# One gate group for the first two chunks, and first fills on VectorE, in a gated-recurrence and channel-mixer kernel

## The chip, the cores and the metric

The kernel runs on one core of a Trainium2 chip. The core has a matrix engine (TensorE, PE in the profile, its weight loads PEld), three elementwise engines (VectorE or DVE, ScalarE or ACT, GpSimd or POOL) and a queue engine (SyncE or SP) that here only issues DMAs. The metric is the device time in microseconds; a kernel's time is the median of its runs.

## The reference

Two blocks, one after the other, in float32 with the weights in float64.

```
# q, k, v, a_re, a_im: (B=4, H=8, S=768, D=48)
mag = sqrt(a_re^2 + a_im^2);  a = (a_re + i a_im) * min(mag, 0.999) / (mag + 1e-6)
for t in range(S):                       # per batch and head; state is D x D, complex
    S_re, S_im = a[t] * (S_re + i S_im)  # row d of the state is multiplied by a[t, d]
    S_re += outer(k[t], v[t])
    y[t] = q[t] @ S_re
x = y as (B, S, H*D = 384)
u = x + (x^T @ U @ V)^T                  # U: 768 x 32, V: 32 x 768, mixes along the sequence
out = u + relu(u @ w_ch1) @ w_ch2        # w_ch1: 384 x 1536, w_ch2: 1536 x 384
```

## The kernel before

The sequence is cut in chunks of 128 steps: six to a batch, 24 in all (`NT`). The recurrence inside a chunk becomes matrix products once the running products of the gates are known, so the work of a chunk has these parts.

- **Gates** (`gates`). From a_re and a_im ScalarE and VectorE make the logarithm of each gate's magnitude (`magnitudes`, 11 ScalarE and 5 VectorE operations on 384 values per chunk) and two exponentials of its sums over the chunk (`within`: one TensorE product `es ps`, two Exp). `totals` makes the decays of blocks of steps (`of_blocks`: TensorE products `tot`, one Exp into E, then four DMAs on SP's queue that copy E into T). `turns` and `angles` make the phases (Arctan, a TensorE prefix sum `ph`, rounding into F; chunk i of the first batch also adds the last row of F of chunk i-1) and `waves` the cosines and sines (`cs`).
- **Prep** (`prep`). VectorE multiplies q and k by the exponentials (L669) and by cs (L673, into QKC); TensorE transposes (L682) and ScalarE copies out (L685) into QK.
- **Chain** (`chain`). TensorE products of 32 columns (`inner`, L716), VectorE copies under a mask (L722) and multiplications of QK by T (L735 through the helper at L329), corners, state updates (G, GM) and y. This is ranked as "levels" and "rest".
- **Mixer** (`mixer`). When the six chunks of a batch are done, the mix along the sequence, and then for each pair of chunks the product with w_ch1 (`up`, L916), Relu, and the product with w_ch2 (`down`).

**Weights.** They arrive as float64. `single` takes one of 13 pieces (w1: 0 to 5, U and V: 6, w2: 7 to 12) through one of two raw buffers (a ring: pieces take them in their order), six VectorE operations (L486 to L496) and one accumulating DMA from GpSimd's queue (L499). `up` on the first half of its columns needs pieces 0 to 2, on the second half 3 to 5; the mix needs piece 6, `down` the rest.

**Groups and tables.** Gates are made in groups of chunks: before, chunk 0 alone, chunk 1 alone, then pairs. ScalarE's Exp and Ln need one activation table, Arctan and Sin another, so every group loads two (`switch`, L323, L1201 and L1210). In the plan a load writes a name that every table operation reads: it waits for all table operations declared ahead of it, and those declared after it wait for the load. The totals of chunk 0 are put off to the next group's Exp table (`later`, L1206). A group's gate tiles (ar, ai, x, y, n, z) are one buffer each, 768 values wide, handed from group to group; chunk 1's inputs therefore cannot be loaded before chunk 0's last reader is done.

**Order.** Every operation is declared with an engine, a cost, a rank and what it reads and writes. `Plan.order` then fixes one order for each engine: of the operations that are ready in its model, the one with the lowest rank goes first. Ranks come from the table `URGENCY` (per part and chunk), and for loads from a formula. SP and GpSimd's queues are in order too, so a DMA that waits holds back those behind it. Where TensorE has nothing to do before the first mixer, the plan puts in 128-wide products of the identity, called `spare` (L1232); they compute nothing that is used.

**First fills.** Ahead of the planned work GpSimd fills tiles with constants: total, ident, GL (L386), QKC (L392), three T (L400), two AT and two DG (L406, L407). VectorE fills only six columns of one value (L364). After that GpSimd makes `mid` (L415) and `total` (L435) from the loaded `prefix`.

Of the kernel before, what the change touches and what calls it, by code (L numbers as in the profile page):

```python
# [22 lines left out]
GC = 2  # L23
# [3 lines left out]
    "w1": {0: 577.09, 1: -1319.32, 2: 484.43, 3: -236.69, 4: 471.82, 5: -1058.73, 6: 187.51},  # L27
    "w2": {0: -111.09, 2: 522.21, 4: 896.97, 6: -52.37, 8: 604.14, 10: 640.8, 12: -317.28},
    "gates": {0: -265.04, 1: 268.17, 2: 43.76, 4: -996.63, 6: 89.37, 8: 509.61, 10: -55.71, 12: 809.99, 14: -95.12,
        16: 160.61, 18: -122.91, 20: -425.54, 22: -1729.17},  # L30
    "angles": {0: -126.72, 1: -84.17, 2: -1567.87, 4: -1150.68, 6: -325.13, 8: 105.31, 10: 61.73, 12: 732.88,
        14: -1148.2, 16: 655.25, 18: 538.84, 20: -116.45, 22: 233.15},
    "prep": {0: -1639.87, 1: -367.99, 2: -1022.47, 3: -12.47, 4: -106.92, 5: -436, 6: -74.87, 7: 260.1, 8: -1682.29,
        9: 278.7, 10: 47.08, 11: 569.46, 12: -1452.21, 13: -249.3, 14: -287.97, 15: -363.52, 16: -269.7,
        17: -1664.43, 18: -240.93, 19: 153, 20: -1089.48, 21: -198.95, 22: -127.5, 23: 757.32},
    "levels": {0: 731.75, 1: -318.03, 2: 17.02, 3: -430.68, 4: -436.08, 5: -170.38, 6: 221.56, 7: 124.72, 8: -1567.59,
        9: -1453.16, 10: -1698.36, 11: -60.78, 12: 502.58, 13: 523.21, 14: -1475.59, 15: 515.81, 16: -1265.88,
        17: 487.77, 18: -263.92, 19: 16.81, 20: 723.89, 21: -1759.83, 22: -1111.46, 23: -160.12},
    "rest": {0: 468.93, 1: -1086.12, 2: 24.25, 3: -218.54, 4: -1119.41, 5: -346.92, 6: 0.68, 7: -1700.8, 8: 681.55,
        9: -376.72, 10: -229.72, 11: -305.85, 12: -1069.62, 13: 601.71, 14: -282.72, 15: 204.95, 16: 59.77,  # L40
        17: 552.08, 18: -62.45, 19: 466.03, 20: -1105.96, 21: -351.77, 22: -1688.33, 23: 463.92},
# [147 lines left out]
def kernel(  # L189
# [47 lines left out]
    GROUPS = [(0, 1), (1, 2)] + [(n, n + GC) for n in range(2, NT, GC)]  # L237
    NG = len(GROUPS)

    PAIRED = 6  # L240
# [5 lines left out]
    AT_ONCE = (0, 1, 2, 3)  # L246
# [145 lines left out]
    nc.gpsimd.memset(QKC, 0.0)  # L392
# [5 lines left out]
    for n in range(3):  # L398
        TS.append(singles.tile([DQ, GC, H * NTOT], FP, name="T%d" % n))
        nc.gpsimd.memset(TS[n], 1.0)  # L400
    for n in range(3):
        VP.append(singles.tile([128, H, D], FP, name="VP%d" % n))
    for n in range(2):
        AT.append(singles.tile([128, H, HC], FP, name="AT%d" % n))
        DG.append(singles.tile([128, H, BLK], FP, name="DG%d" % n))
        nc.gpsimd.memset(AT[n], 0.0)  # L406
        nc.gpsimd.memset(DG[n], 0.0)  # L407
# [37 lines left out]
    def load_a(g):  # L445
        lo, hi = GROUPS[g]
        for nm, src in (("ar", a_re), ("ai", a_im)):
            for i in range(lo, hi):
                SP(c_dma(DM), ("load", (0, 0.5, 3)[g] if g < 3 else lo + 3), lambda nm=nm, src=src, i=i: nc.sync.dma_start(
                    out=get(nm, g)[:, i - lo], in_=rows(src, i)), writes=[(nm, g, i)])  # L450
# [80 lines left out]
    def gates(g):  # L531


        lo, hi = GROUPS[g]
        W = (hi - lo) * DM
        R1, R2 = ("gates", lo), ("angles", lo)
        ca, cd = c_act(W), c_dve(W)
        x, y, l, n, z, ar, ai = names = [(nm, g) for nm in ("x", "y", "l", "n", "z", "ar", "ai")]

        def t(b):  # L540
            a = get(*b)
            return (a.rearrange("p c h d -> p (c h d)") if b[0][0] == "a" else a)[:, 0:W]

        def of(b, i):
            return get(*b)[:, (i - lo) * DM:(i - lo + 1) * DM]

        def magnitudes():
            ring(l, "GL", GL)
            ACT(ca, R1, lambda: act(t(x), t(ar), AF.Square), [ar], [x])
            ACT(ca, R1, lambda: act(t(y), t(ai), AF.Square), [ai], [y])  # L550
            DVE(cd, R1, lambda: add(t(x), t(x), t(y)), [y], [x])
            DVE(c_one(W), R1, lambda: nc.vector.tensor_scalar(out=t(x), in0=t(x), scalar1=M2LO, scalar2=M2HI, op0=OP.max,
                                                              op1=OP.min), [], [x])
            ACT(ca, R1, lambda: act(t(n), t(ar), AF.Abs), [ar], [n])
            table(ca, R1, lambda: act(t(l), t(x), AF.Ln), [x], [l])
            table(ca, R1, lambda: act(t(x), t(l), AF.Exp, scale=0.5), [l], [x])
            DVE(cd, R1, lambda: add(t(x), t(x), t(n)), [n], [x])
            table(ca, R1, lambda: act(t(y), t(l), AF.Exp, scale=-0.5, bias=leps), [l], [y])
            table(ca, R1, lambda: act(t(y), t(y), AF.Ln, bias=1.0), [], [y])

            ACT(ca, R1, lambda: act(t(l), t(l), AF.Relu, scale=-0.5, bias=lmax), [], [l])
            DVE(cd, R1, lambda: nc.vector.scalar_tensor_tensor(out=t(l), in0=t(l), scalar=LNMAX, in1=t(y), op0=OP.subtract,
                                                               op1=OP.add), [y], [l])
            table(ca, R1, lambda: act(t(x), t(x), AF.Ln), [], [x])
            table(ca, R1, lambda: act(t(x), t(x), AF.Exp, scale=-1.0), [], [x])
            DVE(cd, R1, lambda: mul(t(x), t(x), t(ai)), [ai], [x])
            ACT(ca, R1, lambda: act(t(n), t(ar), AF.Sign, bias=tiny), [ar], [n])
            for i in range(lo, hi):
                within(i)

        def within(i):
# [4 lines left out]
               [l, ("mid", 0)], [ps, ("sums", g, i)], takes=[es], steps=2)  # L576
# [3 lines left out]
        def totals():  # L580
# [3 lines left out]
            for i in range(lo, hi):  # L584
                of_blocks(i)
# [6 lines left out]
        def of_blocks(i):  # L592
# [15 lines left out]
        def turns():  # L608

            table(ca, R2, lambda: act(t(x), t(x), AF.Arctan), [], [x])  # L610
            DVE(cd, R2, lambda: nc.vector.scalar_tensor_tensor(out=t(z), in0=t(x), scalar=math.pi / 4, in1=t(n),  # L611
                                                               op0=OP.subtract, op1=OP.mult), [x, n], [z])
            ACT(ca, R2, lambda: act(t(z), t(z), AF.Identity, scale=1.0 / math.pi, bias=fourth), [], [z])
            for i in range(lo, hi):
                angles(i)

        def angles(i):
# [6 lines left out]
            first = i < NCH  # L624
            if where(i)[1] > 0 and not first:
# [5 lines left out]
            carry = first and i > 0  # L631
# [9 lines left out]
        def waves():  # L641
            cs = ("cs", g)
            buffer(cs, "cs", 2, [128, GC, H, 2, D])

            def half(u):
                return get(*cs).rearrange("p c h u d -> p (c h) u d")[:, 0:W // D, u]
            fs = [("F", i) for i in range(lo, hi)]
            ft = heads(F.rearrange("p c m -> p (c m)")[:, lo % GC * DM:lo % GC * DM + W])
            ACT(ca, R2, lambda: act(half(0), ft, AF.Abs), fs, [cs + (0,)])
            table(ca, R2, lambda: act(half(1), ft, AF.Sin, scale=2.0 * math.pi), fs, [cs + (1,)])  # L650
            table(ca, R2, lambda: act(half(0), half(0), AF.Sin, scale=-2.0 * math.pi, bias=quarter), [], [cs + (0,)])
# [9 lines left out]
    def prep(i):  # L661
        R1 = "prep", i
        g = group_of(i)
        qk, QK = ("qk", i), ("QK", i)
        buffer(QK, "QK", 3, [DQ, 2, H, CH])
# [4 lines left out]
        for u in range(2):  # L670
# [4 lines left out]
                [qk, ("cs", g)], [qkc])  # L675
# [521 lines left out]
    for g in range(NG):  # L1197
# [8 lines left out]
        if g:  # L1206
            totals()
        else:
            later = [totals]
# [78 lines left out]
```

## Time and profile before

| | |
|---|---|
| runs | 705.47 us median (704.29, 705.47, 705.83) |
| profiled execution | 704.41 us, of which the span from first to last instruction is 702.6 us |
| TensorE | busy 681.1 us (97% of the span), 61.4 us of it `spare` |
| VectorE | busy 540.1 us (77%) |
| ScalarE | busy 418.1 us (60%), 26 table loads of 1283 ns |
| GpSimd | busy 51.8 us (7%) |
| first `up` product | 152.4 us after the span's start |

A row of a group of instructions reads: line, engine, operation, what is written from what, shapes, count, then busy time and mean duration, then the idle time ahead of them and what ended it. A row of the timeline reads: start in us, duration, engine, line, operation, and in brackets how long the engine had been idle and who released it. In a row of windows each stretch has its length, and for each engine the busy time and the instructions; then the granted TensorE clock (1.00 is full), the DMA engines' busy share and GB/s.

### The profile page before, as it was taken

What the parts mean: (1) busy time and instruction counts of PE and PEld (TensorE: products, weight loads), DVE (VectorE), ACT (ScalarE), POOL (GpSimd) and SP (SyncE); (2) the same over time, 40 slices, a digit from 0 to 9 for tenths busy, and PEclk for the clock granted to TensorE, in tenths of its full rate; (3) what the DMA queues carried; (4) which work ended last, traced back from release to release, by engine and by line L of the source; (5) the groups of instructions that cost most, each with busy time, mean ns of one, the idle gap of its engine ahead of it and who ended that gap; (6) DMA issues with size and microseconds to landing.
All of it is one profiled execution on the core that took longest, in us unless ns stands there. A gap on an engine that the chain in (4) does not pass through costs nothing.

```text
span 702.6 us, 27047 instructions
## 1 busy us (share of the span) xinstructions
PE 681.1 (97%) x12148; PEld 601.0 (86%) x12148; DVE 540.1 (77%) x877; ACT 418.1 (60%) x778; POOL 51.8 (7%) x92
## 2 busy tenths in 40 slices
PE   7989998999999999999999999999999999999998
PEld 6877877877688888879888888889999999899997
DVE  5899998888898887759678487879887787455734
ACT  6786987678797687977784953651624415041230
POOL 5110000011000010001000000000000000000000
PEclk9999999799999999999999999999999999999999
DMA  7876855498424343252334032040121000000000
GB/s 185 172 184 149 186 103 141 91 209 176 99 51 90 68 94 76 41 109 53 63 77 93 9 67 59 10 98 26 23 42 35 14 27 17 18 7 24 7 18 22
DMA packets 165267, 53.24 MB, mean 76 GB/s; under 512 B 154080, under 2 KB 160416, under 8 KB 165152
## 3 DMA queue, kind: packets, MB, share of 16 engines
q1 hardware_dynamic: 161072, 42.26, 27.7%
q0 software_dynamic: 4080, 9.27, 5.6%
q8 instruction: 95, 1.56, 0.9%
q14 instruction: 20, 0.16, 0.1%
HBM read 33.59 MB, written 4.72 MB: 55 GB/s over the span
## 4 chain that ended last, share of the span: by engine, by line
PE 79%; ACT 9%; DVE 7%; issue 3%; DMA 1%; SPq 0%; DVEq 0%; ACTq 0%
PE down L1105 21%; PE few L974 12%; PE up L916 12%; PE inner L716 6%; PE tr L682 5%; ACT gate L326 3%; PE dk L802 3%; PE y L841 3%; PE spare L1232 2%; PE ks ps L787 2%; PE down L1062 2%; PE es ps L575 2%; PE ph L632 2%; PE tot L601 2%; PE y L833 2%
## 5 line engine op out<-in xcount | busy, mean ns | idle before, releaser
L329 DVE TENSOR_TENSOR QK<-QK,T 112x1024 f32<-112x1024 f32 x120 | 145.8, 1221 | 6.5 <-PE corners L766 5.3
L916 PE MATMUL up<-uT,w 128*128 128x256 f32 x432 | 98.7, 381 | 0.0
L916 PEld LDWEIGHTS up<-uT,w 128*128 128x128 f32 x432 | 80.7, 190 | 12.0 <-DVE uT L906 0.2
L326 ACT ACTIVATE gate<-gate 128x768 f32<-128x768 f32 (+1 forms) x91 | 71.0, 792 | 6.2 <-DVE gate L611 2.0
L1105 PE MATMUL down<-w,h 128*128 128x192 f32 x396 | 73.2, 330 | 0.0
L982 ACT COPY h<-few 128x512 f32<-128x512 f32 x36 | 20.8, 584 | 85.2 <-PE few L974 85.1
L685 ACT COPY QK<-tr 112x512 f32<-112x512 f32 x96 | 52.0, 588 | 32.6 <-PE tr L682 32.3
L1105 PEld LDWEIGHTS down<-w,h 128*128 128x128 f32 x396 | 63.9, 190 | 2.7 <-issue 1.3
L1232 PE MATMUL spare<-ident 128*128 128x128 f32 x438 | 61.4, 289 | 2.1 <-POOL ident masks.py:199 1.5
L332 DVE TENSOR_TENSOR h<-few,h 128x512 f32<-128x512 f32 x54 | 37.2, 691 | 30.2 <-PE few L974 26.2
L1232 PEld LDWEIGHTS spare<-ident 128*128 128x128 f32 x438 | 55.1, 198 | 5.9 <-issue 1.9
L716 PEld LDWEIGHTS inner<-QK 112*32 112x32 f32 x4608 | 45.9, 110 | 16.4 <-issue 10.7
L716 PE MATMUL inner<-QK 112*32 112x16 f32 (+1 forms) x4608 | 51.2, 190 | 4.9 <-issue 4.5
L682 PE MATMUL tr<-ident,QKC 128*112 128x128 f32 x384 | 51.9, 275 | 1.2 <-ACT QK L685 0.8
L329 DVE TENSOR_TENSOR QKC<-qk,cs 128x768 f32<-128x768 f32 x48 | 45.9, 956 | 9.3 <-PE tr L682 6.6
L332 DVE TENSOR_TENSOR xo<-down,xo 128x192 f32<-128x192 f32 (+1 forms) x79 | 29.8, 388 | 27.0 <-PE down L1105 25.2
L682 PEld LDWEIGHTS tr<-ident,QKC 128*112 128x112 f32 x384 | 42.3, 133 | 6.1 <-ACT QK L685 1.8
L974 PE MATMUL few<-gate,w 128*128 128x128 f32 x336 | 43.1, 277 | 0.0
L1049 POOL DMA_DIRECT2D out_dram<-xo x32 | 17.9, 560 | 338.9 <-DVE xo L332 278.8
L850 ACT COPY xo<-y 64x192 f32<-64x192 f32 x96 | 30.1, 313 | 19.2 <-PE y L841 16.0
L722 DVE COPY_PREDICATED DG<-mask,inner 128x128 f32<-128x128 int32 (+1 forms) x72 | 24.6, 344 | 20.4 <-PE inner L716 20.3
L974 PEld LDWEIGHTS few<-gate,w 128*128 128x128 f32 x336 | 40.0, 192 | 0.3
(131 smaller groups left out, 1272.0 us busy)
## 6 DMA issues: line engine op xcount, KB each, us to landing
stage<-in_moe_w_ch_dram SPq DMA_DIRECT2D x12, 768.0 KB, 6.5
gate<-in_a_re_dram SPq DMA_DIRECT2D x24, 192.0 KB, 3.2
gate<-in_a_im_dram SPq DMA_DIRECT2D x24, 192.0 KB, 4.3
qk<-in_q_dram SPq DMA_DIRECT2D x24, 192.0 KB, 4.0
qk<-in_k_dram SPq DMA_DIRECT2D x24, 192.0 KB, 4.4
VP<-in_v_dram SPq DMA_DIRECT2D x24, 192.0 KB, 3.3
w<-stage POOLq DMA_DIRECT2D x12, 384.0 KB, 5.7
T<-E SPq DMA_DIRECT2D x44, 96.0 KB, 2.5
```

The source lines that it names most:

```text
L326: return nc.scalar.activation(out=o, in_=i, func=f, **kw)
L329: nc.vector.tensor_tensor(out=o, in0=a, in1=b, op=OP.mult)
L332: nc.vector.tensor_tensor(out=o, in0=a, in1=b, op=OP.add)
L682: nc.tensor.transpose(out=get(*ps)[0:DQ, j], in_=get(*qkc)[:, hh * HH + j].rearrange("p u d -> p (u d)")[:, 0:DQ], identity=ident)
L685: ACT(c_act(HH * CH) - 0.05, R1, lambda u=u, hh=hh, ps=ps: nc.scalar.copy(out=get(*QK)[:, u, hh * HH:(hh + 1) * HH], in_=get(*ps)[0:DQ]), ...
L716: nc.tensor.matmul(out=get(*ps)[js, h], lhsT=k_of(h)[:, js], rhs=part(q_of(h)[:, js], "p"), start=True, stop=True, tile_position=(0, j * BLK))
L722: nc.vector.copy_predicated(out=to, mask=part(mask[:, n], "p").unsqueeze(1).to_broadcast(list(to.shape)), data=a if hf < 8 else a.rearrang ...
L850: ACT(c_act(HH * D), RR, lambda r=r, u=u: nc.scalar.copy(out=get(*xi).rearrange("p (a u d) -> p a u d", u=2, d=D)[r * HC:(r + 1) * HC, :, ...
L916: nc.tensor.matmul(out=get(*ps)[:, e], lhsT=w1[:, f, (ff + e) * 128:(ff + e + 1) * 128], rhs=get(*uT)[:, f], start=(f == 0), stop=(f == KD ...
L974: nc.tensor.matmul(out=get(*ps)[:, q], lhsT=w()[:, q * 128:(q + 1) * 128], rhs=v[0](), start=(n == 0 and q == 0), stop=True, skip_group_ch ...
L1105: nc.tensor.matmul(out=get(*to)[:, part], lhsT=x(j), rhs=y[:, j], start=(first and j == 0), stop=(j == KH - 1), skip_group_check=not first)
L1232: nc.tensor.matmul(out=spare[0], lhsT=ident, rhs=ident, start=True, stop=True)
```

## The change

- `GROUPS` are pairs from the start: chunks 0 and 1 are one group. `PARTS` cuts this first group into two parts of one chunk, so that its operations keep their width of 384; all other groups are one part of two chunks. `magnitudes`, `turns` and `waves` loop over the parts.
- The group's totals come ahead of its second table for the first group as well; nothing is put off.
- `PAIRED` and `AT_ONCE` move by one, since group numbers do.
- Inputs a_re and a_im of chunk 1 get the load rank 0.05 (chunk 0 has 0, the prefix table 0.1, the first weight piece 1).
- The fills of QKC, the three T, two AT and two DG go to VectorE.
- All ranks in `URGENCY` are new.

```diff
 URGENCY = {
-    "w1": {0: 577.09, 1: -1319.32, 2: 484.43, 3: -236.69, 4: 471.82, 5: -1058.73, 6: 187.51},
...
-    "gates": {0: -265.04, 1: 268.17, 2: 43.76, 4: -996.63, 6: 89.37, 8: 509.61, 10: -55.71, 12: 809.99, 14: -95.12,
...
-    "prep": {0: -1639.87, 1: -367.99, 2: -1022.47, 3: -12.47, 4: -106.92, 5: -436, 6: -74.87, 7: 260.1, 8: -1682.29,
...
-    "levels": {0: 731.75, 1: -318.03, 2: 17.02, 3: -430.68, 4: -436.08, 5: -170.38, 6: 221.56, 7: 124.72, 8: -1567.59,
...
-    "rest": {0: 468.93, 1: -1086.12, 2: 24.25, 3: -218.54, 4: -1119.41, 5: -346.92, 6: 0.68, 7: -1700.8, 8: 681.55,
...
+    "w1": {0: -1281.04, 1: -1220.88, 2: -1207.45, 3: 315.61, 4: 369.7, 5: 444.04, 6: 70.95},
...
+    "gates": {0: 253.11, 1: -1390.93, 2: -0.7, 4: -1280.16, 6: 565.76, 8: -1068.17, 10: -187.84, 12: -54.04, 14: 550.2,
...
+    "prep": {0: -1294.88, 1: 125.6, 2: -26.13, 3: 96.73, 4: 102.92, 5: 146.86, 6: 553.65, 7: 283.9, 8: 120.02,
...
+    "levels": {0: 201.22, 1: 294.56, 2: -15.94, 3: 207.38, 4: -1236.01, 5: 275.3, 6: 572.46, 7: 14.34, 8: -1057.92,
...
+    "rest": {0: 93.55, 1: 47.27, 2: 273.41, 3: 257.67, 4: -1050.04, 5: -1068.08, 6: -1240.77, 7: -1208.87, 8: -1033.73,
...
-    GROUPS = [(0, 1), (1, 2)] + [(n, n + GC) for n in range(2, NT, GC)]
+    GROUPS = [(n, n + GC) for n in range(0, NT, GC)]
+    PARTS = [[(n, n + 1) for n in range(GC)]] + [[g] for g in GROUPS[1:]]
...
-    PAIRED = 6
+    PAIRED = 5
...
-    AT_ONCE = (0, 1, 2, 3)
+    AT_ONCE = (0, 1, 2)
...
-    nc.gpsimd.memset(QKC, 0.0)
+    nc.vector.memset(QKC, 0.0)
...
-        nc.gpsimd.memset(TS[n], 1.0)
+        nc.vector.memset(TS[n], 1.0)
...
-        nc.gpsimd.memset(AT[n], 0.0)
-        nc.gpsimd.memset(DG[n], 0.0)
+        nc.vector.memset(AT[n], 0.0)
+        nc.vector.memset(DG[n], 0.0)
...
-                SP(c_dma(DM), ("load", (0, 0.5, 3)[g] if g < 3 else lo + 3), lambda nm=nm, src=src, i=i: nc.sync.dma_start(
+                SP(c_dma(DM), ("load", i / 20 if g == 0 else 3 if g == 1 else lo + 3), lambda nm=nm, src=src, i=i: nc.sync.dma_start(
...
         def magnitudes():
             ring(l, "GL", GL)
...
+            for part in PARTS[g]:
+                magnitudes_of(*part)
+
+        def magnitudes_of(lo, hi):
+            t, R1, W = t_of(lo, hi), ("gates", lo), (hi - lo) * DM
+            ca, cd = c_act(W), c_dve(W)
+            X, Y, L, N = (b + (lo,) for b in (x, y, l, n))
+            AR, AI = ([b + (i,) for i in range(lo, hi)] for b in (ar, ai))
+            ACT(ca, R1, lambda: act(t(x), t(ar), AF.Square), AR, [X])
...
         def turns():
...
+            for part in PARTS[g]:
+                turns_of(*part)
+
+        def turns_of(lo, hi):
+            t, R2, W = t_of(lo, hi), ("angles", lo), (hi - lo) * DM
...
         def waves():
-            cs = ("cs", g)
-            buffer(cs, "cs", 2, [128, GC, H, 2, D])
+            buffer(("cs", g), "cs", 2, [128, GC, H, 2, D])
+            for part in PARTS[g]:
+                waves_of(*part)
...
         magnitudes()
-        if g:
-            totals()
-        else:
-            later = [totals]
+        totals()
         switch(rank, trigs)
         turns()
```

## The prediction

> **What bounds the kernel.** First the page's busy row, then the windows by stage, to see where TensorE's busy time is real.
>
> ```profile
> PE 681.1 (97%) x12148; PEld 601.0 (86%) x12148; DVE 540.1 (77%) x877; ACT 418.1 (60%) x778; POOL 51.8 (7%) x92
> L1232 PE MATMUL spare<-ident 128*128 128x128 f32 x438 | 61.4, 289 | 2.1 <-POOL ident masks.py:199 1.5
> 0.00:20.00 20.00, 14.99 (x107) 13.37 (x108) 11.05 (x25) 12.41 (x23) 10.65 (x33) 0.91 0.82 190
> 20.00:40.00 20.00, 18.43 (x323) 15.79 (x322) 17.41 (x26) 14.38 (x26) 1.72 (x2) 1.00 0.74 157
> 40.00:60.00 20.00, 17.66 (x355) 15.22 (x354) 19.66 (x29) 17.45 (x31) 1.12 (x1) 1.00 0.71 192
> 60.00:80.00 20.00, 19.25 (x384) 16.31 (x383) 19.03 (x28) 15.40 (x27) 1.72 (x2) 1.00 0.83 177
> 80.00:100.00 20.00, 18.71 (x506) 15.14 (x508) 19.50 (x30) 16.82 (x34) 0.86 (x1) 1.00 0.64 130
> 100.00:120.00 20.00, 15.92 (x518) 14.02 (x512) 17.67 (x28) 17.65 (x31) 0.86 (x1) 1.00 0.56 137
> 120.00:140.00 20.00, 19.56 (x531) 16.89 (x533) 16.57 (x24) 10.96 (x28) 0.00 (x0) 0.74 0.37 80
> 140.00:152.40 12.40, 12.26 (x171) 9.23 (x168) 11.14 (x19) 8.42 (x14) 2.89 (x3) 1.00 0.84 174
> 152.40:250.00 97.60, 97.28 (x1690) 78.41 (x1690) 84.94 (x120) 76.67 (x133) 7.49 (x10) 1.00 0.49 105
> ```
>
> The columns are PE, PEld, DVE, ACT, POOL, clock, DMA share, GB/s. Two stages show. From the first `up` (152.4 us) TensorE is never short of work: 97.28 of the next 97.60 us. Before it TensorE is busy 136.8 of 152.4 us (the first eight windows summed), but all 61.4 us of `spare` lie there, so only 75.4 us are work and 77 us are not. The time therefore moves almost one for one with the moment the first mixer may start, corrected for real TensorE work that moves across that moment. In this first stage VectorE is busy 132.0 us and idle 20.4: idle 8.95 before 20 us, 1.8 between 40 and 100 (97% busy), 5.8 between 100 and 140. VectorE is its bound, with ScalarE second (81.7 of 100 us between 20 and 120).
>
> Now the beginning, in the timeline of VectorE, GpSimd and ScalarE.
>
> ```profile
> 5.24 0.56 DVE L332 TENSOR_TENSOR gate<-gate 128x384 f32<-128x384 f32 x1 [4.22 <-ACT gate L326]
> 5.83 1.73 DVE L552 TENSOR_SCALAR gate<-gate 128x384 f32<-128x384 f32 x1
> 19.85 0.36 DVE L552 TENSOR_SCALAR gate<-gate 128x384 f32<-128x384 f32 x1
> 3.17 2.73 POOL L400 MEMSET T<- 112x1024 f32 x3
> 7.04 0.31 POOL L407 MEMSET DG<- 128x256 f32 x1
> 13.59 1.28 ACT L323 ACT_TABLE_LOAD   x1
> 20.84 1.28 ACT L323 ACT_TABLE_LOAD   x1
> 32.82 1.28 ACT L323 ACT_TABLE_LOAD   x1
> 42.08 1.28 ACT L323 ACT_TABLE_LOAD   x1
> ```
>
> The same clamp (L552) takes 1.73 us at 5.83 and 0.36 at 19.85; the long one lies under GpSimd's fills and ends as they do (7.35). Chunk 0 gets its cosines at 20.83, chunk 1 only at 42.06, after two further table loads; VectorE is idle while only chunk 0's short operations are at hand.
>
> **The change, part by part.**
>
> *Fills.* Eight fills leave GpSimd (0.95 + 2.73 + 2 x 0.52 + 2 x 0.31 = 5.34 us of rows) and begin on VectorE at 1.0, behind its six column fills. Three T, QKC, two AT and two DG are 4x1024 + 2x512 + 2x256 = 5632 elements per partition. The trace has no large VectorE fill, only 59 ns for one element. From below, the nearest single-input row: the clamp takes 0.36 us on 384 and 0.55 on 768, 0.49 ns per element, so 2.8 us + 8 x 0.06 = 3.3; VectorE is then free at 4.3, before its first addition at 5.24: no cost. From above, the Trainium skill, "VectorE: DVE Perf Modes", section "Zero memsets can be issued as uint32 (trn2)": a memset takes one cycle per element whatever the type, and the same page's specifications give 0.96 GHz: 5.87 + 0.48 = 6.3 us (an estimate from that page), the slope of the two-input rows here too (0.56 at 384, 0.96 at 768: 1.04 ns). VectorE is then free at 7.3 and the addition starts 2.1 late. I take 6.3, since a fill is the page's own case. The stall of L552 goes (-1.37) with its cause, so chunk 0's clamp ends at 7.3 + 0.56 + 0.36 = 8.2 against 7.56: +0.7 by the page, -1.4 by the row. On GpSimd the 5.3 us buy nothing: `mid` and `total` need the prefix table, whose load now comes behind chunk 1's inputs. The DMAs move 185 GB/s at first; 4 x 192 + 64 KB take 4.6 us, plus 2.5 for issue and flight, so it lands near 7, where `mid` starts today (7.32).
>
> *Loads.* On SP's queue chunk 1's two inputs pass prefix, mask, weight piece 0, q, k and v of chunk 0; each of these lands 384 KB, or 2.1 us, later. Piece 0 (first VectorE step at 11.45) starts near 13; VectorE has chunk 1's five gate operations for that gap. q and k are used from 14.45 and were issued by 4.1: covered. Chunk 1's inputs, issued at 11.25 and 12.49 behind a buffer wait, land near 6.5 instead. Without that wait, piece 1 and chunk 1's q, k, v behind it can go early as well, as far as the DMA rate allows. Four issues T<-E fewer on SP (2.55 us of rows at 22.59): SP is no bound, zero.
>
> *Gates in one group.* Two table loads less. The rows give 1.28 each, with the next activation at once (13.59 + 1.28 = 14.87, Arctan at 14.88): 2.6 us. "ScalarE: Activation LUTs", section "What ACT_TABLE_LOAD costs", would have 2.66 each with a drain, 5.3 in all; no drain shows, so I take 2.6. The order is what matters: chunk 0's Arctan now waits for chunk 1's magnitudes and totals. Under the Exp table one chunk has 7.1 us of ScalarE rows, two 14.2, less about 0.09 for each of 28 overlapping starts: 11.7. Six of the 28 fit ahead of the clamp at 8.2; the other 22 at 0.43 take 9.4, plus about 1 for TensorE's products: the second table at 18.7, Arctan at 20.0 instead of 14.88. Chunk 0's cosines come at 26.0, +5.2. Queued behind are Arctan of both chunks on ScalarE, chunk 0's products with cs on VectorE, its transposes on TensorE (which has `spare` there). What hides the 5.2 is weight conversion: one piece is 0.55 + 0.55 + 0.56 + 0.96 + 0.56 + 0.96 = 4.14 us of VectorE, and pieces 0 to 2 have very low ranks. Without that cover chunk 0 alone would cost up to 5.2. On the other side chunk 1 has its cosines near 27.5 (42.06), and the pair 2, 3 gets its table near 27.5 (42.08): every later group may be some 14 us earlier.
>
> *What VectorE gains.* To 20 us it does 11.05 - 1.37 = 9.7 us of work now. Then: 20 - 0.8 (start) - 6.3 (fills) - 1.5 (waits, as now between 11 and 20) = 11.4. Gain 1.7. Between 20 and 40 it idles 2.59, of which 1.17 at 23.53 waits for chunk 1's magnitudes and 0.49 at 39.16 for the next pair's; two chunks at hand should fill half of that: 0.8.
>
> *New ranks.* Now `gates` 6 (89) beats `levels` 0 (732) and `rest` 0 (469). In the new table gates, prep and levels of chunk 6 (554 to 572) rank behind nearly all work of chunks 0 to 5 (at most 295). Before the first mixer VectorE today does chunk 6 and 7's gates (0.96, 0.56, 0.96, 0.95, 0.95, 0.96 = 5.3) and first products (1.9), 7.2 us, which may now go later. TensorE's part of it moves behind too (`es ps`, `tot`, `ph`: about 4.6 at full clock), so 2.6 at most is gained; I take half, 1.3.
>
> Sum: -1.7 - 0.8 - 1.3 = -3.8, against the profiled execution's 704.41 (span 702.6 and 1.8 around it): 700.6. The median of the runs lies 1.06 higher: 701.7. With the quick fills it would be about 1 less.
>
> **Rivals.**
> *Bigger gain.* The gates' 14 us lead reaches the end of chunk 5. By 143 us VectorE has 108 us of work that the mixer needs; with 13 to 20 us of idle this could end near 121 to 128. For it: between 100 and 140 us the idle time and a 3.1 us stop of TensorE at 116 (released by nothing shown; the granted clock is then 0.74 from 120 to 140) come from the order. Against: 97% busy from 40 to 100, and real TensorE work moves with it. A mixer 12 us earlier, half of it real work moved: -6 more than the start's, -9 in all: 696.5.
> *Slower: late weights.* w1's pieces 3 to 5 rank 316 to 444, behind all of chunks 0 to 5, and piece 6 (71) must follow them through the two raw buffers; the mix needs piece 6. Today pieces 0, 2 and 4 rank as late (577, 484, 472), and yet w1 is done at 72, in VectorE's gaps. With two chunks always at hand these gaps may go. If all four pieces are left when chunk 5 ends, 3 x 4.14 + 2.5 of VectorE and 9.4 for the landing of piece 6 are 24 us, of which another chunk's TensorE work (75.4 / 6 = 12.6) covers half: +12; two pieces left, +4. It decides from the point where piece 6's conversion ends after chunk 5's y. 709 to 717, say 711.
> *No change.* VectorE is 97% busy behind the start, so what is won in the first 40 us is only filled with weights that wait for nobody: 705.5.
>
> **How the numbers follow.** Forecast 0.43, bigger gain 0.15, no change 0.12, late weights 0.30. About what a measurement can tell from no change is 0.2% (1.4 us): faster 0.58, same 0.12, slower 0.30. The forecast's own range is 698.5 to 704, its ends the two prices of the fills and full or no gain of the ranks. The whole range takes in the bigger gain with some below it and the slower case up to two thirds: 693 to 713, with about 0.06 left below and 0.10 above.
>
> **What would show it.** VectorE's fills as rows of 1.1 us (page) or 0.6 on 1024; L552 at 0.36 everywhere; 24 table loads, the second near 18 to 20 us, the third near 27; chunk 1's QKC before 32; `spare` below 61.4 us and the first `up` near 148; `up` still without gaps. Wrong would be: the first `up` later than 152, with L496 of pieces 3 to 5 after 120 us; or the first `up` earlier but gaps in TensorE behind 160, where there are next to none now, because chunk 6's work was put off too far.

## The result, and the profile after

The kernel after takes 698.27 us (median of four runs, 696.75 to 701.21), the one before 705.65 beside it (704.29 to 708.86): a ratio of 0.9894, 95% interval 0.9846 to 0.9942. A second measurement on another occasion gave 0.9909 (0.9883 to 0.9936). The forecast was 701.7 with a range of 693 to 713: the direction is right and the time lies in the range, but the gain of 7.4 us is twice the 3.8 that were worked out.

The profiled execution takes 697.56 us, its span is 695.8 (before: 704.41 and 702.6). First the busy row and the `spare` group of the page of after.

```profile
PE 671.9 (97%) x12116; PEld 592.7 (85%) x12116; DVE 542.3 (78%) x885; ACT 416.3 (60%) x776; POOL 47.5 (7%) x84
L1252 PE MATMUL spare<-ident 128*128 128x128 f32 x406 | 57.5, 288 | 1.8 <-POOL ident masks.py:199 1.5
```

The windows by stage of after, with the columns of the rows shown of before (PE, PEld, DVE, ACT, POOL, clock, DMA share, GB/s):

```profile
0.00:20.00 20.00, 17.00 (x140) 15.93 (x141) 15.19 (x34) 15.00 (x31) 5.78 (x24) 1.00 0.74 176
20.00:40.00 20.00, 17.16 (x302) 14.64 (x301) 16.54 (x25) 17.20 (x29) 1.94 (x2) 1.00 1.00 219
40.00:60.00 20.00, 18.78 (x439) 15.48 (x438) 19.97 (x28) 15.43 (x26) 0.86 (x1) 1.00 0.69 146
60.00:80.00 20.00, 18.68 (x461) 16.24 (x461) 19.98 (x29) 17.93 (x35) 0.86 (x1) 1.00 0.62 127
80.00:100.00 20.00, 18.39 (x498) 15.46 (x490) 19.82 (x32) 16.24 (x33) 0.86 (x1) 1.00 0.54 117
100.00:120.00 20.00, 17.38 (x674) 15.65 (x674) 18.73 (x28) 9.08 (x22) 1.71 (x2) 1.00 0.59 112
120.00:140.00 20.00, 19.22 (x340) 14.36 (x329) 17.36 (x28) 17.96 (x33) 0.86 (x1) 1.00 0.71 180
140.71:152.40 11.69, 11.69 (x56) 10.11 (x55) 9.03 (x15) 5.71 (x10) 2.83 (x3) 1.00 0.89 204
152.40:250.00 97.60, 96.07 (x1755) 77.16 (x1754) 88.86 (x126) 80.49 (x141) 8.29 (x11) 1.00 0.50 106
```

The first `up` now stands at 140.71 us. Before, its row starts at 152.24, so it is 11.5 us earlier; the windows of before are cut at 152.40, 0.16 behind it. VectorE (third number) is full between 40 and 100 us to 0.23 us, where it idled 1.8 before. From 152.4 to 250, where TensorE was busy 97.28 of 97.60 us, it is now busy 96.07: a part of the gain is given back there.

The account follows from two windows on each side of the first `up`, of before and then of after:

```profile
0.00:152.40 152.40, 136.77 (x2855) 115.97 (x2856) 132.04 (x201) 113.49 (x209) 19.83 (x43) 0.96 0.68 154
152.40:702.60 550.20, 544.37 (x9294) 485.06 (x9293) 408.09 (x676) 304.61 (x570) 31.94 (x49) 1.00 0.25 54
```

```profile
0.00:140.71 140.71, 127.31 (x2821) 108.44 (x2821) 128.29 (x199) 109.32 (x204) 12.85 (x32) 1.00 0.70 155
140.71:695.80 555.09, 544.64 (x9298) 484.24 (x9296) 414.00 (x687) 306.95 (x573) 34.69 (x52) 1.00 0.26 57
```

Ahead of the first `up`, VectorE's busy time falls by 3.75 us and its idle time by 7.9 (20.36 to 12.42): 11.7 in all. Behind it TensorE has the same work (544.4 and 544.6 us, 9294 and 9298 products), but the stretch is 4.9 us longer: TensorE's idle time there goes from 5.8 to 10.5. So 11.7 - 4.9 = 6.8 us of span, in one profiled execution of each kernel.

The lead can be followed along the chain. The last state update of chunks 1 to 5 (GM<-GM,dk) starts at 88.52, 101.01, 115.28, 132.49 and 141.30 us before, and at 77.87, 90.63, 105.30, 119.46 and 128.34 after: 10.7, 10.4, 10.0, 13.0 and 13.0 us earlier. Ten of these are there by chunk 3. The other three come where TensorE stops in before, at 116 us, and its granted clock falls to 0.74 behind that. VectorE's three longest waits behind 40 us of before are all there, 5.1 us in all:

```profile
119.62 0.45 DVE L722 COPY_PREDICATED DG<-mask,inner 128x256 f32<-128x256 int32 x1 [2.18 <-PE inner L716]
127.16 0.29 DVE L722 COPY_PREDICATED DG<-mask,inner 128x128 f32<-128x128 int32 x1 [1.02 <-PE inner L716]
132.49 0.56 DVE L332 TENSOR_TENSOR GM<-GM,dk 112x384 f32<-112x384 f32 x1 [1.90 <-PE dk L802]
```

After has no stop over 1 us between 100 and 140 us, and its longest wait of VectorE there is 1.07 us. From chunk 5's last update to the first `up`, 1.4 us are lost again (10.9 us before, 12.4 after).

The beginning, in the timeline of VectorE and of ScalarE after (start, duration, engine, line, operation):

```profile
1.20 0.91 DVE L393 MEMSET QKC<- 128x1024 f32 x1 [0.18 <-issue]
2.27 0.91 DVE L401 MEMSET T<- 112x1024 f32 x1 [0.16 <-issue]
5.39 0.48 DVE L407 MEMSET AT<- 128x512 f32 x1
6.69 0.27 DVE L408 MEMSET DG<- 128x256 f32 x1
6.88 0.49 DVE L333 TENSOR_TENSOR gate<-gate 128x384 f32<-128x384 f32 x1
7.41 0.43 DVE L560 TENSOR_SCALAR gate<-gate 128x384 f32<-128x384 f32 x1
...
18.63 1.28 ACT L324 ACT_TABLE_LOAD   x1
24.74 0.60 ACT L327 ACTIVATE cs<-cs,quarter 128x384 f32<-128x384 f32 x1
27.81 0.60 ACT L327 ACTIVATE cs<-cs,quarter 128x384 f32<-128x384 f32 x1
29.38 1.28 ACT L324 ACT_TABLE_LOAD   x1
```

The fills end at 6.96, the clamp (L560) takes 0.43 us in place of 1.73 and ends at 7.84 (7.56 before). The cosines of chunk 0 are done at 25.3, those of chunk 1 at 28.4 (42.06 before), and the table for the gates of chunks 2 and 3 is loaded at 29.4, where before it was 42.1.

### The profile page after: what moved, and what is told of

It reads as the page before. It is cut to its first block, busy times and chain, and to the rows that moved or that the text cites. A ratio compares the mean times of both kernels' runs of the same rounds, so it can differ in the third digit from the quotient of the medians.

```text
span 695.8 us, 26968 instructions
## 1 busy us (share of the span) xinstructions
PE 671.9 (97%) x12116; PEld 592.7 (85%) x12116; DVE 542.3 (78%) x885; ACT 416.3 (60%) x776; POOL 47.5 (7%) x84
## 4 chain that ended last, share of the span: by engine, by line
PE 78%; ACT 10%; DVE 8%; issue 3%; DMA 1%; SPq 0%; DVEq 0%; ACTq 0%
PE down L1128 20%; PE few L997 12%; PE up L939 10%; PE inner L739 6%; PE tr L705 6%; ACT gate L327 4%; PE y L864 3%; PE dk L825 3%; PE down L1085 2%; PE ph L650 2%; PE es ps L583 2%; PE ks ps L810 2%; PE spare L1252 2%; PE tot L612 2%; DVE QK L330 2%
## 5 line engine op out<-in xcount | busy, mean ns | idle before, releaser
L739 PEld LDWEIGHTS inner<-QK 112*32 112x32 f32 x4608 | 45.4, 109 | 20.2 <-issue 15.2
L333 DVE TENSOR_TENSOR h<-few,h 128x512 f32<-128x512 f32 x54 | 37.1, 690 | 30.6 <-PE few L997 28.1
L1252 PE MATMUL spare<-ident 128*128 128x128 f32 x406 | 57.5, 288 | 1.8 <-POOL ident masks.py:199 1.5
L330 DVE TENSOR_TENSOR QKC<-qk,cs 128x768 f32<-128x768 f32 x48 | 45.7, 953 | 14.9 <-PE tr L705 13.4
L705 PE MATMUL tr<-ident,QKC 128*112 128x128 f32 x384 | 54.2, 276 | 2.9 <-ACT QK L708 1.1
L1252 PEld LDWEIGHTS spare<-ident 128*128 128x128 f32 x406 | 51.8, 199 | 5.7 <-POOL ident masks.py:199 1.5
L333 DVE TENSOR_TENSOR xo<-down,xo 128x192 f32<-128x192 f32 (+1 forms) x79 | 29.6, 385 | 28.5 <-PE down L1128 28.4
L705 PEld LDWEIGHTS tr<-ident,QKC 128*112 128x112 f32 x384 | 42.1, 133 | 11.2 <-issue 3.1
L873 ACT COPY xo<-y 64x192 f32<-64x192 f32 x96 | 30.0, 313 | 19.1 <-PE y L864 17.7
L1072 POOL DMA_DIRECT2D out_dram<-xo x32 | 18.7, 586 | 320.0 <-DVE xo L333 288.2
L1128 PE MATMUL down<-stage 128*128 128x192 f32 x198 | 36.8, 329 | 0.1
```

What stands on the lines that cost most here:

```text
L330: nc.vector.tensor_tensor(out=o, in0=a, in1=b, op=OP.mult)
L333: nc.vector.tensor_tensor(out=o, in0=a, in1=b, op=OP.add)
L705: nc.tensor.transpose(out=get(*ps)[0:DQ, j], in_=get(*qkc)[:, hh * HH + j].rearrange("p u d -> p (u d)")[:, 0:DQ], identity=ident)
L739: nc.tensor.matmul(out=get(*ps)[js, h], lhsT=k_of(h)[:, js], rhs=part(q_of(h)[:, js], "p"), start=True, stop=True, tile_position=(0, j * BLK))
L873: ACT(c_act(HH * D), RR, lambda r=r, u=u: nc.scalar.copy(out=get(*xi).rearrange("p (a u d) -> p a u d", u=2, d=D)[r * HC:(r + 1) * HC, :, ...
L1128: nc.tensor.matmul(out=get(*to)[:, part], lhsT=x(j), rhs=y[:, j], start=(first and j == 0), stop=(j == KH - 1), skip_group_check=not first)
```

## The experiments

Five questions: what the fills are worth; whether grouping or the new ranks carry the gain; which part of the ranks does; whether a few microseconds on ScalarE at the beginning reach the first `up`; and what takes 4.9 us back behind it. No run changes what is computed. This table holds what the questions are read from. "Work" and "idle" are VectorE's, ahead of the first `up`; "behind" is the span from there to the end; these four come from one profiled execution each. The medians come from several occasions, on which before took 703.56 to 705.65 us; a ratio compares with before on the same one.

| kernel | first `up` | work | idle | behind | median |
|---|---|---|---|---|---|
| before, cut at 152.4 | 152.2 | 132.0 | 20.4 | 550.2 | 705.65 |
| after | 140.7 | 128.3 | 12.4 | 555.1 | 698.27 |
| before, fills on VectorE | 155.1 | 135.6 | 19.5 | 550.5 | 704.94 |
| after, fills on GpSimd | 142.2 | 124.5 | 17.7 | 555.7 | 696.82 |
| before, new ranks | 175.1 | 144.6 | 30.4 | 573.9 | 747.63 |
| after, old ranks | 169.7 | 144.1 | 25.6 | 556.0 | 731.69 |
| after, old ranks for weights | 155.0 | 136.5 | 18.5 | 560.8 | 718.09 |
| after, old ranks for chunks 6, 7 | 203.9 | 180.4 | 23.5 | 540.2 | 747.27 |
| after, old ranks for chunks 8 on | 140.8 | 128.4 | 12.4 | 574.0 | 717.2 |
| after, 2nd and 3rd table load thrice | 148.6 | 128.7 | 19.9 | 555.2 | 703.0 |
| after, 2nd load thrice | 145.7 | 128.4 | 17.2 | 555.8 | 701.85 |
| after, 3rd load thrice | 143.7 | 128.5 | 15.2 | 556.3 | 702.68 |
| after, inner products split | 141.7 | 128.6 | 13.1 | 555.7 | 699.46 |
| after, once more | 140.4 | 128.5 | 12.0 | 554.4 | 699.01 |

### The fills

Before, with the fills on VectorE; and after, with the fills on GpSimd as they were. The order of every engine is otherwise that of the kernel it starts from.

```diff
-    nc.gpsimd.memset(QKC, 0.0)
+    nc.vector.memset(QKC, 0.0)
...
-        nc.gpsimd.memset(TS[n], 1.0)
+        nc.vector.memset(TS[n], 1.0)
...
-        nc.gpsimd.memset(AT[n], 0.0)
-        nc.gpsimd.memset(DG[n], 0.0)
+        nc.vector.memset(AT[n], 0.0)
+        nc.vector.memset(DG[n], 0.0)
```

> The kernel before with the eight fills on VectorE, all engines' planned orders being the same. The prediction's account of this part: the clamp loses its 1.37 us stall, but chunk 0's first addition waits for the fills until 6.9 us, so its logarithm starts 0.1 to 0.7 us later than at 7.66 us; 705 to 707 us, no measurable change. A rival account, in which GpSimd's early freedom counts (mid and total ready sooner): 703 to 704.5 us.

> The kernel after with the eight fills back on GpSimd, all planned orders the same. If the fills hardly count: within 1 us of the kernel after, 697.5 to 699.5 us. Rival: with two chunks in the first group there are two clamps to be held up by GpSimd's fills, and mid and total come behind both chunks' magnitudes, so the second table load slips by 1.5 to 3 us and the time by as much, 699.5 to 701.5 us.

Measured: 704.94 us, ratio to before 0.999 (0.9968 to 1.0012), and 696.82, ratio to before 0.9884 (0.9844 to 0.9923; with the fills on VectorE 0.9894). Put in or taken out, the fills make no difference that can be measured. VectorE's busy time ahead of the first `up` moves by 3.6 and 3.8 us, as 5.1 us of fills less 1.4 of stall say; they lie in time in which VectorE waits anyway: its idle time in the first 40 us falls by 3.3 us in both. The first `up` of the profiled executions stands 2.9 and 1.5 us later than in the kernels they start from, though the medians don't: with the fills on VectorE before, that execution took 707.44 us, 2.5 over its median, with a TensorE stop of 2.31 us at 43 that before's lacks. A difference of up to 3 us at the first `up` of a single profile is therefore no finding by itself.

### The group or the ranks

Before, with only the table of ranks of after; and after, with only the table of before. The second has the group, the parts, the load order and the fills.

```diff
 URGENCY = {
-    "w1": {0: 577.09, 1: -1319.32, 2: 484.43, 3: -236.69, 4: 471.82, 5: -1058.73, 6: 187.51},
...
+    "w1": {0: -1281.04, 1: -1220.88, 2: -1207.45, 3: 315.61, 4: 369.7, 5: 444.04, 6: 70.95},
...
```

> The kernel before, with nothing changed but the rank table, which is that of the kernel after. Theory A (the group gives the gain: its 14 us lead for all later gates keeps VectorE supplied): the ranks alone give little, 704 to 707 us, first up product at 150 us or later, VectorE still idle some 20 us before it. Theory B (the ranks give it, by putting chunk 6 and 7 and late weight pieces behind chunks 0 to 5): 698 to 701 us, first up at 141 to 145 us, with one weight piece less converted before it than in the kernel before.

> The kernel after with the rank table of the kernel before. Theory A: most of the gain is there without the ranks, 699 to 702 us, first up at 141 to 146 us, VectorE idle 12 to 15 us before it. Theory B: 704 to 708 us, first up at 150 us or later; the group alone only brings chunk 1 forward at chunk 0's cost.

Measured: 747.63 us, ratio 1.0603 (1.0554 to 1.0652), and 731.69, ratio 1.0382 (1.0343 to 1.042). Neither the theory that the group carries the gain nor the one that the ranks do stands: each alone is 4 to 6% slower, and together they are 1.1% faster. The table shows where: with ranks that don't belong to the grouping VectorE has 144 us of work ahead of the first `up` in place of 128 to 132, and idles 26 to 30 us in place of 12 to 20. The new ranks alone also lose 24 us behind the first `up` (573.9 against 550.2). The group alone does not even bring the lead forward: with the old ranks the second and third table load come at 19.7 and 30.7, as after, but the fourth at 52.9 and the fifth at 67.1, where after has 45.7 and 58.1.

### Parts of the ranks

After, each time with one part of the table as before: the pieces of w1 with U and V; chunks 6 and 7; chunks 8 to 23.

```diff
-    "w1": {0: -1281.04, 1: -1220.88, 2: -1207.45, 3: 315.61, 4: 369.7, 5: 444.04, 6: 70.95},
+    "w1": {0: 577.09, 1: -1319.32, 2: 484.43, 3: -236.69, 4: 471.82, 5: -1058.73, 6: 187.51},
```

> The kernel after with only the ranks of the w1 pieces and of U and V as before: piece 0 then ranks at 577 and not at -1281, and all other pieces follow it through the ring. Theory F (the prediction's cover: weight conversion at the head of VectorE's queue hides the wait for chunk 0's cosines, and put anywhere else it is on the path): VectorE idles some 8 us more before 30 us, first up near 147 to 150, 702 to 706. Rival G (VectorE's sum of work counts and not its order): first up within 2 us of 140.7, 697 to 700. Rival H (w1's new ranks were themselves too late and their old ones end sooner): first up before 139, under 696.

718.09 us, ratio 1.0194 (1.0153 to 1.0235), first `up` at 155.0: later still than theory F had it. But its reason isn't what the windows show: up to 40 us VectorE is busy 31.2 us, after 31.7. The additional 8 us of work and 6 of idle come later.

```diff
-    "gates": {0: 253.11, 1: -1390.93, 2: -0.7, 4: -1280.16, 6: 565.76, 8: -1068.17, 10: -187.84, 12: -54.04, 14: 550.2,
+    "gates": {0: 253.11, 1: -1390.93, 2: -0.7, 4: -1280.16, 6: 89.37, 8: -1068.17, 10: -187.84, 12: -54.04, 14: 550.2,
...
-    "prep": {0: -1294.88, 1: 125.6, 2: -26.13, 3: 96.73, 4: 102.92, 5: 146.86, 6: 553.65, 7: 283.9, 8: 120.02,
+    "prep": {0: -1294.88, 1: 125.6, 2: -26.13, 3: 96.73, 4: 102.92, 5: 146.86, 6: -74.87, 7: 260.1, 8: 120.02,
...
```

> The kernel after with only the ranks of chunks 6 and 7 (gates, angles, prep, levels, rest) as before, which brings their gates and first products ahead of the first mixer again. The prediction's step: VectorE has 7.2 us more to do before the first up, TensorE 4.6, so the time rises by 1.3 (at most 2.6): first up near 147, 699.6. Rival D (TensorE's part is less than thought, so that nearly the whole delay of the first up counts): first up near 147, 702 to 704. Rival E (this work only fills waits of VectorE, which has 12 us idle there): first up within 1 us of 140.7, 697.5 to 699.

747.27 us, ratio 1.0614 (1.0571 to 1.0656); the first `up` at 203.9. No theory had anything of this size. The window behind the first `up`:

```profile
203.90:744.10 540.20, 527.75 (x8650) 470.52 (x8648) 362.00 (x616) 255.38 (x493) 25.95 (x43) 1.00 0.19 42
```

VectorE has 362.0 us of work left there, after has 414.0: 52 us of it went ahead of the first mixer, not the 7.2 of the prediction. ScalarE has 13 table loads ahead of the first `up` here, after has 9: two more groups of gates were begun. The table of ranks suggests why: the gate tiles are handed from group to group, so once chunks 6 and 7 have had them, chunk 8's gates (-1068) and angles (-1315) are ready, with ranks below those of chunk 5's chain (levels 275). In the timeline additions and clamps of gates of a later group (168 to 178 us) and weight pieces (up to 184) do stand among the last operations of chunk 5, whose last state update comes at 182.5 (128 in after). The rank of chunks 6 and 7 was thus no term of 1.3 us, but works like a dam that holds back what is ranked low behind it; no run changed chunk 8's ranks together with these, so the dam is read from ranks and timeline.

```diff
-    "gates": {0: 253.11, 1: -1390.93, 2: -0.7, 4: -1280.16, 6: 565.76, 8: -1068.17, 10: -187.84, 12: -54.04, 14: 550.2,
+    "gates": {0: 253.11, 1: -1390.93, 2: -0.7, 4: -1280.16, 6: 565.76, 8: 509.61, 10: -55.71, 12: 809.99, 14: -95.12,
...
```

> The kernel after with the ranks of gates, angles, prep, levels and rest of chunks 8 to 23 as in the kernel before; those of chunks 0 to 7 and of the weights stay new. After, the first up came 11.5 us earlier but the span is only 6.8 shorter: TensorE stands idle some 4.7 us more behind the first up. Theory P (the loss lies in the new ranks of the later chunks): first up stays at 140 to 142 us, TensorE's idle time behind it falls from about 10 to about 6 us, 693 to 695 us. Theory Q (the loss comes with an earlier first mixer, whatever the later ranks): first up at 140 to 142, idle time stays near 10, 697 to 699. Theory R (a table of ranks is fitted as a whole, and foreign ranks cost in any part of it): new waits of TensorE behind 160 us, over 702.

717.2 us, ratio 1.0186 (1.0149 to 1.0224). The first `up` is where it was (140.8), and all 19 us are lost behind it: TensorE's busy time there is 555.0 us (544.6), its idle time 19.0 (10.5). Theory R holds, and the old ranks don't take back the 4.9 us.

### A few microseconds on ScalarE

After, with a table load made three times in its place (by way of the other table); each engine keeps its order.

```diff
-        switch(rank, exps)
+        switch(rank, *((exps, trigs, exps) if g == 1 else (exps,)))
...
-        switch(rank, trigs)
+        switch(rank, *((trigs, exps, trigs) if g == 0 else (trigs,)))
```

> The kernel after with the second and the third table load made three times (four loads more in all, each pair before 31 us); the orders of all engines are the same otherwise. By the row of 1.28 us without a drain each place costs ScalarE 2.56 us, by the page's 2.66 us each it costs 5.3. Theory K (ScalarE's chain of the first two groups is on the path, as the prediction's order of steps has it): the first cosines come 2.6 later, chunks 2 and 3 get theirs 5.1 later, first up 2.5 to 5 us later, 700.5 to 703. Rival L (weight conversion covers it all): first up within 1 us of 140.7, 697.5 to 699. With the page's price the first two figures are 5.3 and 10.6, and the time over 703.

703.0 us, ratio 0.999 (0.996 to 1.002); the first `up` at 148.6, 7.9 later than after and beyond the 2.5 to 5 of theory K. With 5.1 us more on ScalarE the gain over before can no longer be measured. Then each of the two places alone:

> The kernel after with only its second table load (the one ahead of the first Arctan, at 18.6 us) made three times; the order of every engine is the same otherwise. Made three times at the second and third load, 5.1 us more on ScalarE put the first up 7.9 us later and the span 8.0. Here 2.56 us more, ahead of the cosines of chunks 0 and 1 and of the third load too. Theory K2 (a delay of the first cosines runs on through ScalarE's order into all later groups): first up 2.5 to 4 us later (143 to 145), 700.5 to 702.5. Rival M (only the later pair's gates count, the first cosines have weight conversion as their cover): first up within 1 us of 140.7, 697.5 to 699.

> The kernel after with only its third table load (ahead of the gates of chunks 2 and 3, at 29.4 us) made three times; the order of every engine is the same otherwise. ScalarE has 2.56 us more ahead of the gates of chunks 2 and 3, and the cosines of chunks 0 and 1 are as early as after. Theory K2 (the moment at which each next pair gets its gates sets the pace to the end of chunk 5): first up 2.5 to 4 us later (143 to 145), 700.5 to 702.5. Rival N (what counts is when chunks 0 and 1 have their cosines, and the pair 2, 3 has time in hand): first up within 1 us of 140.7, 697.5 to 699.

Beside after's 699.01 us (ratio 0.9909) on the same chip: 701.85, ratio 0.9957 (0.9941 to 0.9973), and 702.68, ratio 0.9975 (0.9952 to 0.9999). In the medians the second load costs 2.8 us and the third 3.7, where each adds 2.56 to ScalarE; both together cost about 5.7 by the ratios. In the profiled executions, against that run's first `up` at 140.43, it comes 5.2, 3.2 and 8.2 us later, with granted clocks down to 0.83 in some stretches that after's lacks, so these figures say less than the medians. Rivals L, M and N fall. K2's size stands for the second load (701.85 in 700.5 to 702.5) and is just missed by the third. Its way isn't the only one for the third: VectorE's waits for the transposes of QKC grow there from 2.5 to 4.8 us, that for a gate from 0.2 to 1.5, so the copies of transposes on ScalarE are held up as well as the next pair's gates. The three loads in one row of ScalarE's timeline, with the second load thrice; then VectorE's waits between 18 and 45 us, of the same kernel and of after:

```profile
18.68 3.86 ACT L324 ACT_TABLE_LOAD   x3
```

```profile
DVE gate L629 <- ACT gate L327: 3.3, 1, 3.3
DVE QKC L330 <- PE tr L705: 2.5, 2, 1.3
```

```profile
DVE QKC L330 <- PE tr L705: 2.5, 2, 1.3
DVE gate L629 <- ACT gate L327: 0.7, 1, 0.7
```

A load takes 1.29 us without a drain. VectorE's wait for the first Arctan grows from 0.7 to 3.3 us, by all that was added, and the timeline of the kernel with the second load thrice shows why weight conversion is no cover:

```profile
23.11 1.03 DVE L629 SCALAR_TENSOR_TENSOR gate<-gate 128x384 f32<-128x384 f32 x2 [3.27 <-ACT gate L327]
24.05 0.56 DVE L487 TENSOR_SCALAR stage<-stage 128x768 uint32<-128x768 uint32 x1
24.64 0.56 DVE L489 TENSOR_SCALAR stage<-stage 128x768 f32<-128x768 f32 x1
```

The next weight piece (L487) stands right behind the operation that waits, and the order is fixed. From there to the first `up` VectorE is busy 112.2 of 121.6 us, and little makes up for it.

### What is given back behind the first `up`

TensorE's waits behind the first `up`, of before and then of after (line, who is waited for; us in total, times, longest):

```profile
PE inner L716 <- issue: 1.0, 1, 1.0
PE uTp L904 <- DVE xo L332: 0.6, 3, 0.2
PE ph L632 <- ACT QK L685: 0.3, 1, 0.3
PE ks ps L787 <- DVE QK L329: 0.2, 1, 0.2
```

```profile
PE inner L739 <- issue: 4.3, 3, 2.4
PE tr L705 <- ACT QK L708: 0.9, 2, 0.7
PE uTp L927 <- DVE xo L333: 0.6, 3, 0.3
PE dk L825 <- ACT ks L812: 0.4, 1, 0.4
```

The largest are three stops amid `inner` that no other engine releases, at 262, 411 and 522 us. At these places one or two long products of the mixer were put between the two halves of the inner products:

```diff
-    for n in plan.order():
-        (plan.ops[n][4] if n >= 0 else idle)()
+    for x, moved in ((458, [3]), (621, [2]), (748, [1, 2])):
+        between[pe[x]] = [pe[x + m] for m in moved]
...
+        if n in between:
+            halves[n][0]()
+            for m in between[n]:
+                plan.ops[m][4]()
+            halves[n][1]()
```

> The kernel after with three places of TensorE's order changed behind the first up: where two chunks' inner products (128 of 16 or 32 columns in a row, at 262, 411.5 and 522.7 us) are followed or broken by a stop of 0.93, 0.99 and 2.36 us that nothing releases, one or two long products of the mixer from just behind are put between the two halves. All ranks and the order of the other engines stay. Theory S (the stops come where too many short products stand in a row): the three stops go, behind the first up TensorE's waits fall from 6.9 to 3 us, and the time is 2.5 to 4 us less than after's: 694 to 696. Rival T (the stop is owed whatever stands there, or goes to the next short products): same within 1 us of after, first up unchanged.

> The kernel after once more, on the same chip as the three others: 698 us, first up at 140.7, a ratio of 0.985 to 0.994 to before. It is the measure for the split of the inner products, which is to be told from it by 0.4%.

699.46 us, ratio to before 0.9922 (0.9903 to 0.994); after beside it 699.01, ratio 0.9909 (0.9883 to 0.9936). The longest stop in after, and the same place in the split kernel:

```profile
522.67 1.24 PE L739 MATMUL inner<-QK 112*32 112x16 f32 x124
526.27 0.24 PE L739 MATMUL inner<-QK 112*32 112x16 f32 x4 [2.36 <-issue]
```

```profile
524.36 0.73 PE L739 MATMUL inner<-QK 112*32 112x16 f32 x64
525.02 1.16 PE L997 MATMUL few<-uT,gate 128*128 128x128 f32 x8
526.02 1.06 PE L997 MATMUL few<-gate,w 128*128 128x128 f32 x8
527.01 1.00 PE L739 MATMUL inner<-QK 112*32 112x16 f32 x64
...
530.14 1.16 PE L997 MATMUL few<-gate 128*128 128x128 f32 x8 [1.04 <-DVE h L333]
```

Theory S is right on the stops: all three are gone. It is wrong on the time. The moved products are now missing further on: TensorE waits 1.04 us for VectorE at 530, and for QKC and QK elsewhere; the stretch behind the first `up` is 555.7 us, as long as ever. That stretch is 554.4 to 556.3 us in every kernel with after's order, whether its first `up` stands at 140.4 or at 148.6. So the 4.9 us belong to this order and not to an earlier first mixer, and the stops were not what they depend on. The order includes that VectorE has 5.9 us more work behind the first `up` (414.0 against 408.1); no run separates this from the ranks of the later chunks. Which wait they do depend on stays open. None of the kernels measures faster than after beyond its uncertainty.

## Why the prediction was half right

**The bound and the stage** were right: TensorE's work behind the first `up` is unchanged, and the time followed the moment of the first `up`, though 4.9 of the 11.7 us were lost behind it. That the time landed in the range owes much to luck: a lead three times the forecast one met a loss that wasn't forecast at all.

**Fills.** 6.3 us by the Trainium skill ("VectorE: DVE Perf Modes", section "Zero memsets can be issued as uint32 (trn2)"), 3.3 by the row: 5.8 measured (1.20 to 6.96), with 1.07 us from one fill of 1024 to the next, as the page's one cycle per element at 0.96 GHz gives; those of 512 stand 0.49 from the next, where it gives 0.53. Taking the page was right. The clamp ends at 7.84 (8.2 expected); its stall is gone, and `mid` starts at 6.62 (about 7). No value for the time, as runs in both directions show.

**Loads.** The first weight step starts at 14.04 (near 13).

**Tables.** Second load 18.63 (18.7), Arctan 19.93 (20.0), chunk 0's cosines 25.3 (26.0), chunk 1's 28.4 (27.5), third load 29.38 (27.5), 24 loads. A load is 1.28 to 1.29 us with no drain, as the row had it; the 2.66 us of the Trainium skill ("ScalarE: Activation LUTs", section "What ACT_TABLE_LOAD costs") appear in no run here. This part was sized well.

**What VectorE gains at the start: 1.7 + 0.8.** Wrong in size and place. Work other than fills and stall done by 20 us went from 9.7 to 10.1 us: 0.4. Between 20 and 40 the idle time grew from 2.59 to 3.46: a loss of 0.9, two waits of 1.30 and 1.24 for chunk 1's transposes among it. The first 40 us thus gave -0.5, not 2.5.

**Zero behind 40 us.** This step failed. The prediction let the lead end where it had filled VectorE's gaps before 40 us, and kept the 14 us for a rival. VectorE's idle time behind 40 us fell from 8.8 to 4.1 us: 4.7 gained where nothing was forecast. But these are not gaps that earlier gates filled: 5.1 of the 8.8 are the three waits for TensorE at and behind its stop at 116 us. Between 40 and 100 us only 1.6 were won. Why after has no such stop is open; the orders differ there. That the beginning does reach the end of the stage is shown by the table loads made thrice: 2.56 us of ScalarE cost 2.8 and 3.7 us of time. The table loads keep their lead too: the first for chunks 4 and 5 comes at 58.10 (70.24 before), that for 6 and 7 at 94.26 (102.89). By the same runs weight conversion was no cover to count on: it hides a wait only where the order has put it ahead of what waits.

**New ranks: 7.2 us of VectorE put off, brought down to 1.3.** In size this is the largest miss. By counting the instructions on both sides, VectorE has 7.5 us less ahead of the first `up` (fills and stall apart), as the windows say too. But this is one weight piece and the last step of another (5.3 us), one addition and one clamp of gates (1.6) and one step of F (0.6), not the gates and first products of chunks 6 and 7: that the 7.2 agrees is luck. And the term set against it, 4.6 us of TensorE's `es ps`, `tot` and `ph` moving too, did not occur: `es ps` has 16 products ahead in both, and only two of 16 `ph` moved. In VectorE's sum the term was worth 7.5; no run isolates it.

The sum at the first `up` is then 0.4 - 0.9 + 4.7 + 7.5 = 11.7, where the prediction had 3.8. Behind it the prediction had nothing, and lost 4.9.

**The rivals.** "Bigger gain" named a first mixer 12 us earlier (11.5 measured) and 696.5 us, which is nearer to the measured 698.27 than the forecast is (1.8 and 3.4 off). It had also named the stop at 116 us and the clock behind it as owed to the order. Its discount was wrong in kind: not real TensorE work moved, but idle time behind. "Late weights" did not decide: UV's conversion ends near 104 us, some 24 before the last state update of chunk 5. "No change" was refuted by its own argument: a VectorE that is 97% busy passes a delay on rather than swallowing it.

**What would show it.** `spare` fell to 57.5, QKC of chunk 1 came at 30.6 and 32.8 (before 32 expected, half missed), the first `up` at 140.7 and not near 148. The warning sign named there, gaps in TensorE behind 160 us, did appear in small.

**Not isolated.** TensorE's real work ahead of the first `up` took 5.6 us less in the profile after (127.31 - 57.5 = 69.8 against 136.77 - 61.4 = 75.4) at all but equal counts; before ran at a granted clock of 0.74 from 120 to 140 us. No run changes the clock alone, but the runs of the last measurement, in which after gains 5.8 us, can be compared at equal mean clock: at 0.998 before takes 703.67 to 704.82 us (four runs) and after 698.23 (one), at 0.995 704.84 (one) and 699.79 and 700.83. About 4.5 to 6 us of difference are left, so the mean clock explains little of the gain, as far as so few runs say.

## What to carry to other kernels

Where an order is fixed ahead of time and fitted as a whole, grouping and ranks are one change: here every part taken alone or taken back, the fills apart, left the kernel 2 to 6% slower than before, so neither half has a worth of its own, and a low rank costs not only its own work but also all that it sets free. If the bounding engine is full from a moment on, a delay before that moment can go to the end of the stage about one for one (2.56 us cost 2.8 and 3.7 here); "97% busy" speaks for that, not against. And read what the bounding engine's few waits are for: here most were for a stop of another engine. Work counts as a cover only if it stands ahead of the waiting instruction in that engine's queue.

## What was not expected of the hardware

- TensorE stops amid long runs of short products, for 0.9 to 2.4 us in after and up to 4.94 in other orders, released by no other engine; rows of 128 products (as the profile counts them) of 16 or 32 columns had it in three places, and with long products put between the halves all three stops went.
- A stretch of lower granted clock followed each such stop of 2.6 us or more. In before, a row of TensorE's timeline, and the window of 110 to 130 us:

```profile
119.11 0.45 PE L716 MATMUL inner<-QK 112*32 112x32 f32 x30 [3.10 <-issue]
```

```profile
110.00:130.00 20.00, 16.32 (x491) 14.13 (x481) 16.14 (x23) 12.03 (x26) 0.41 (x1) 0.76 0.48 130
```

  After has no stop over 1 us there, and a clock of 1.00. The kernel with old ranks for the weights stops for 2.59 us up to 130.66 and has 0.54 from 130 to 140; before with new ranks stops for 4.94 up to 143.20 and has 0.66 from 140 to 150. The stops of 2.87 (before with the fills on VectorE), 3.65 (after with old ranks) and 3.99 us (old ranks for chunks 6 and 7) go with 0.59, 0.83 and 0.77 in the next or the same 10 us. Shorter ones differ: after's 2.36 us at 526 is followed by no drop, the 2.33 at the same place with the third load thrice by 0.83. No run changed a stop alone in the first stage, so a cause is not shown.
- Large fills on VectorE stand 0.16 us apart, in which nothing that the profile shows holds them: 0.91 us of each 1.07 are busy.
